# Filling the score operands in an attention-plus-MoE kernel: partition-to-partition DMAs replaced by VectorE copies

## The chip, the cores and the metric

The kernel runs on one core of a Trainium2 chip. The core has a matrix engine (TensorE, PE in the profile, with its weight loads listed as PEld), a vector engine (VectorE, DVE), a scalar engine (ScalarE, ACT), a general one (GpSimd, POOL) and SyncE (SP), which here only issues DMAs. Each engine works through its own queue in order. Sixteen DMA engines move data between HBM and the on-chip memory SBUF, or inside SBUF; matmul results land in PSUM. The metric is the device time of one execution in microseconds.

## The reference

For each of 4 x 8 heads, 768 queries of 64 numbers attend to keys in chunks of 32. A chunk's upper bound for a query comes from the chunk's smallest and largest key values, and only the six best chunks take part. The result goes through a dense two-layer network plus one of eight experts:

```
k_min = np.min(k_chunks, axis=3)
k_max = np.max(k_chunks, axis=3)
ub = np.sum(np.maximum(q[:, :, :, None, :] * k_min[:, :, None, :, :], q[:, :, :, None, :] * k_max[:, :, None, :, :]), axis=-1)
...
top_chunks = np.argsort(ub, axis=-1)[..., -top_k:]
scores = scale * np.matmul(q, k.transpose(0, 1, 3, 2))
...
mask = sel & (pos[:, None] >= pos[None, :])
scores = np.where(mask, scores, -1000000000.0)
...
h_dense = np.maximum(x @ w1_dense, 0.0)
y_dense = h_dense @ w2_dense
logits = x @ w_gate
expert_idx = np.argmax(logits, axis=1)
...
    h = np.maximum(x[mask] @ w1[e], 0.0)
    y_moe[mask] = gate_w[mask, None] * (h @ w2[e])
return (y_dense + y_moe).astype(np.float32)
```

## The kernel before, in words

Two heads of one batch make a pair, and there are 16 pairs. Head 0 of the pair has its 64 numbers on partitions 0 to 63 and head 1 on 64 to 127, since the two heads are transposed together. The masking of unchosen chunks is done inside the score matmul: it contracts over 128 rows, of which 64 carry the head's K and Q; of the other 64, 24 carry on Q's side a flag for each chunk that was not chosen, and on K's side, in 32 rows, -30000 where the key is in that chunk (the constant `exf`) and zeros below. So each head h of a pair has two operands, `kT[i][h]` for K and `rT[i][h]` for Q, in three sets i that take turns (`NB = 3`). In head 0's operands K and Q are on partitions 0 to 63 and the flags' part begins at 64; in head 1's it is the other way round.

A pair is prepared while earlier pairs are computed, in these steps:

- `cast_qk`, `cast_v`: GpSimd turns the loaded fp32 tiles into f16.
- `prep_k` (L379 on): TensorE transposes K into PSUM in six steps (L382); ScalarE copies the result into `kT[i][1]`, which thus holds both heads for a time (L384); VectorE takes the maximum and minimum of each chunk (L388) and builds `kb` (L391, L393), the operand of the upper bounds.
- `prep_q`: TensorE transposes Q (L405); ScalarE writes its positive part to `qp` (L408); VectorE copies it whole into `rT[i][0]` (L409); a DMA brings head 1's half to `rT[i][1]` (L410).
- `prep_kt`: a DMA copies head 0's half of `kT[i][1]` to `kT[i][0]` (L397), and then a second one overwrites rows 0 to 31 of `kT[i][1]` with `exf` (L398). The second has to wait until the first has read, and until the reduces have read.
- `prep_ub`: TensorE makes the upper bounds (L416, L420), using all of `rT[i][0]`; ten MAX8 instructions (L426) find the sixth best, and L428 writes flags.
- `prep_s`: TensorE transposes the flags (L434), VectorE copies them from PSUM to `se` in SBUF (L436), and two DMAs bring head 0's part to `rT[i][0]` (L438) and head 1's to `rT[i][1]` (L439).

The pair's work is then eleven units. In each, `scores` (L448) makes up to 512 columns of scores, ScalarE takes the exponential (L452), GpSimd cuts the diagonal in some units (L454), and `av` (L467) multiplies by V one unit later. `norm` divides and writes the MoE's input `xbig`. Scores of a pair run two units ahead of the loop, so the first scores of pair p + 1 are called at unit 9 of pair p. In the same loop run the fills: from the fifth pair on, pieces of the dense network of the previous batch (L242 to L331) are put between the units.

The loop says at which unit each step is called: `prep_s` of the next pair at unit 2, `prep_k`, `prep_q`, `prep_kt` and `prep_ub` of the pair after it at units 4, 5, 7 and 9. A scheduler in the framework then sets the order on each engine, so the final order is not quite that of the calls; it can be seen by comparing the built programs. SyncE issues all q, k and v loads, the writes of the dense results and the transfers named above through one queue in order. Loads have two buffers per tensor, so a load is issued once the cast two pairs earlier has freed its buffer. Transposes and upper bounds share two PSUM buffers, `pp`.

After the loop the tail gathers tokens by expert in 31 blocks, runs the two expert layers and scatters the rows out (L647 to L695).

Of the kernel before, what the change touches and what calls it, by code (L numbers as in the profile page):

```python
# [10 lines left out]
HF = mybir.dt.float16  # L11
# [6 lines left out]
def kernel(  # L18
# [12 lines left out]
    nc = tc.nc  # L31
    B, H, S, D = q.shape
# [40 lines left out]
    st = [dict() for _ in range(NP)]  # L73
# [23 lines left out]
    NB = 3  # L97
# [4 lines left out]
    kT = [[acst.tile([128, S], HF, name=f"kT{i}_{g}") for g in range(2)] for i in range(NB)]  # L102
    rT = [[acst.tile([128, S], HF, name=f"rT{i}_{g}") for g in range(2)] for i in range(NB)]
# [16 lines left out]
    exf = acst.tile([128, S], HF)  # L120
# [13 lines left out]
                            base=31, pattern=[[-1, S]], channel_multiplier=32)  # L134
    for i in range(NB):
        nc.vector.memset(kT[i][0][64:128], 0.0)
        nc.vector.memset(rT[i][1][0:64], 0.0)
        nc.vector.memset(v16[i][:, :, :, D : D + 1], 1.0)

    def expand(i):  # L140
        nc.scalar.copy(kT[i][0][64:96, :], exf[0:32])


    iom8 = const.tile([128, NT, E], FP)
# [211 lines left out]
    with (  # L356
# [21 lines left out]
        def prep_k(p):  # L378
            s = st[p]  # L379
            pk = pprep.tile([128, S], HF, name="pp")  # L380
            for t in range(NT):
                nc.tensor.transpose(pk[:, t * 128 : (t + 1) * 128], s["k16"][:, t].rearrange("p g d -> p (g d)"), ident)  # L382
            kp = kT[p % NB][1]
            nc.scalar.copy(kp.rearrange("d (T p j) -> d T p j", p=128, j=NJ),  # L384
                           pk.rearrange("d (T j p) -> d T p j", p=128, j=NJ))
            ks = ahead.tile([128, 2, NC], HF, name="ks")
            for i, op in enumerate((ALU.max, ALU.min)):
                nc.vector.tensor_reduce(out=ks[:, i], in_=kp.rearrange("d (c w) -> d c w", w=32), op=op,  # L388
                                        axis=mybir.AxisListType.X)
            s["kb"] = kb = ahead.tile([128, 3, 2, NC], HF, name="kb")  # L390
            nc.vector.tensor_tensor(kb[:, 0:2], ks.unsqueeze(2).to_broadcast([128, 2, 2, NC]),  # L391
                                    hmask.unsqueeze(1).to_broadcast([128, 2, 2, NC]), ALU.mult)
            nc.vector.tensor_tensor(kb[:, 2], ks[:, 1:2].to_broadcast([128, 2, NC]), nmask, ALU.mult)  # L393

        def prep_kt(p):
            k0, k1 = kT[p % NB]
            nc.sync.dma_start(out=k0[0:64], in_=k1[0:64])  # L397
            nc.sync.dma_start(out=k1[0:32], in_=exf[0:32])  # L398

        def prep_q(p):  # L400
            s = st[p]
            pq = pprep.tile([128, S], HF, name="pp")
            pqv = pq.rearrange("d (T h j p) -> d T h j p", h=2, j=NJ, p=64)
            for t in range(NT):
                nc.tensor.transpose(pqv[:, t // NJ, :, t % NJ], s["q16"][:, t].rearrange("p g d -> p (g d)"), ident)  # L405
            s["qp"] = qp = ahead.tile([128, S], HF, name="qp")
            r0, r1 = rT[p % NB]
            nc.scalar.activation(qp, pq, AF.Relu)  # L408
            nc.vector.tensor_copy(r0, pq)  # L409
            nc.sync.dma_start(out=r1[64:128], in_=r0[64:128])  # L410

        def prep_ub(p):

# [16 lines left out]
        def prep_s(p):  # L430
            s = st[p]
            ps = pprep.tile([128, S], HF, name="pp")
            for t in range(NT):
                nc.tensor.transpose(ps[:, t * 128 : (t + 1) * 128], fl[p % 2][:, t], ident)  # L434
            se = ahead.tile([128, S], HF, name="se")
            nc.vector.tensor_copy(se, ps)  # L436
            r0, r1 = rT[p % NB]
            nc.sync.dma_start(out=r0[64:96], in_=se[64:96])  # L438
            nc.sync.dma_start(out=r1[0:32], in_=se[0:32])  # L439

        def scores(p, u):
            s = st[p]
# [40 lines left out]
        for i in range(NB):  # L483
            expand(i)
        cast_qk(0)
        load(2, "kq")
        prep_k(0)
        prep_q(0)
        prep_kt(0)
        cast_v(0)  # L490
        prep_ub(0)
# [3 lines left out]
        load(2, "v")  # L495
        load(3, "v")
        prep_s(0)
        prep_k(1)
        prep_q(1)
        prep_kt(1)  # L500
        cast_qk(2)
        load(4, "kq")
# [19 lines left out]
        for i, (p, u) in enumerate(seq):  # L522
# [4 lines left out]
            if u == 2 and n1 is not None:  # L527
                prep_s(n1)
            if u == 4 and n2 is not None:
                prep_k(n2)  # L530
            if u == 5 and n2 is not None:
                prep_q(n2)
            if u == 7 and n2 is not None:
                prep_kt(n2)
# [214 lines left out]
```

## Time and profile before

The time was 357.41 us, the median of three runs (354.07 to 358.31). The profiled execution has a span of 337.3 us.

| | busy us | share of the span |
|---|---|---|
| PE | 244.4 | 72% |
| ACT | 173.6 | 51% |
| DVE | 165.7 | 49% |
| PEld | 156.8 | 46% |
| POOL | 154.0 | 46% |

| DMA inside SBUF, per pair | size of each | us to landing, median |
|---|---|---|
| kT<-kT, one | 96 KB | 4.6 |
| kT<-exf, one | 48 KB | 2.2 |
| rT<-rT, one | 96 KB | 4.1 |
| rT<-se, two | 48 KB | 5.4 |

Busy shares are averages over a prelude (up to the first score matmul at 23.9 us), the loop over pairs (up to about 227 us) and the tail, which have different limits, so they have to be read by stage. The landing time of a DMA counts from its issue; an engine that needs the data waits for the landing, and a DMA that is issued late lands late. In the lists of waits a line names the engine and line that stood, after the arrow what ended the wait, and then the microseconds in all, the number of waits and the longest. "out<-in" names tiles.

### The profile page before, as it was taken

What the parts mean: (1) busy time and instruction counts of PE and PEld (TensorE: products, weight loads), DVE (VectorE), ACT (ScalarE), POOL (GpSimd) and SP (SyncE); (2) the same over time, 40 slices, a digit from 0 to 9 for tenths busy, and PEclk for the clock granted to TensorE, in tenths of its full rate; (3) what the DMA queues carried; (4) which work ended last, traced back from release to release, by engine and by line L of the source; (5) the groups of instructions that cost most, each with busy time, mean ns of one, the idle gap of its engine ahead of it and who ended that gap; (6) DMA issues with size and microseconds to landing.
All of it is one profiled execution on the core that took longest, in us unless ns stands there. A gap on an engine that the chain in (4) does not pass through costs nothing.

```text
span 337.3 us, 7413 instructions
## 1 busy us (share of the span) xinstructions
PE 244.4 (72%) x2615; PEld 156.8 (46%) x2615; DVE 165.7 (49%) x556; ACT 173.6 (51%) x322; POOL 154.0 (46%) x203
## 2 busy tenths in 40 slices
PE   1418727849949859686686696989874998899882
PEld 1316516628616637454453473655441554444441
DVE  5526606527934447494352586237522454444441
ACT  4318707828817737558373664772341444444441
POOL 6635615436323514443424230110446677777753
PEclk9999958769978969799897989899995999999999
DMA  7976989797998798899994897223869578877760
GB/s 202 276 166 157 185 184 192 143 224 178 195 251 209 180 224 188 176 313 198 248 238 132 151 159 249 76 92 106 277 164 293 171 238 233 244 243 257 227 214 0
DMA packets 80499, 66.23 MB, mean 196 GB/s; under 512 B 30222, under 2 KB 73742, under 8 KB 80464
## 3 DMA queue, kind: packets, MB, share of 16 engines
q1 hardware_dynamic: 65280, 37.17, 40.2%
q0 software_dynamic: 15184, 28.60, 37.8%
q8 instruction: 21, 0.34, 0.4%
q14 instruction: 14, 0.11, 0.1%
HBM read 50.62 MB, written 20.91 MB: 212 GB/s over the span
## 4 chain that ended last, share of the span: by engine, by line
DMA 38%; PE 31%; issue 8%; DVE 8%; POOL 6%; ACT 4%; SPq 3%; POOLq 1%; ACTq 0%; DVEq 0%
DMA rT<-se 24%; PE sp L448 10%; DMA xg<-xd,gi 9%; PE yp L326 6%; POOL xg L647 3%; ACT ex L452 3%; DMA kT<-kT 3%; PE hp L317 3%; PE op L467 2%; POOL out_dram L695 2%; PE yp L691 2%; SPq L88 2%; PE hp L674 2%; PE pp L434 1%; DVE ks L388 1%
## 5 line engine op out<-in xcount | busy, mean ns | idle before, releaser
L452 ACT ACTIVATE ex<-sp 128x512 f16<-128x512 f32 (+1 forms) x176 | 92.6, 591 | 66.3 <-PE sp L448 63.0
L448 PE MATMUL sp<-rT,kT 128*128 128x128 f16 (+3 forms) x384 | 72.3, 297 | 46.8 <-DMA rT<-se 45.7
L454 POOL TENSOR_SCALAR_AFFINE_SELECT ex<-ex 128x512 f16<-128x512 f16 x48 | 31.8, 665 | 84.1 <-ACT ex L452 83.8
L448 PEld LDWEIGHTS <-kT 128*128 128x128 f16 x384 | 32.0, 109 | 56.3 <-issue 50.9
L467 PE MATMUL op<-v,ex 128*128 128x65 f16 x672 | 52.2, 201 | 8.0 <-ACT ex L452 4.7
L467 PEld LDWEIGHTS <-ex 128*128 128x128 f16 x672 | 39.7, 103 | 24.0 <-ACT ex L452 8.5
L695 POOL DMA_INDIRECT out_dram<-yo,si x31 | 31.4, 1013 | 16.0 <-DVE yo L694 9.3
L685 ACT COPY ehT<-tp 128x512 f16<-128x512 f16 x31 | 18.1, 585 | 36.9 <-PE tp L683 36.9
L388 DVE TENSOR_REDUCE ks<-kT 128x24 f16<-128x768 f16 x32 | 29.1, 947 | 14.7 <-ACT kT L384 13.9
L647 POOL DMA_INDIRECT xg<-xd,gi x31 | 29.8, 963 | 12.3 <-issue 5.8
L674 PE MATMUL hp<-we,exT 128*128 x124 | 31.8, 379 | 4.6 <-DVE exT L668 3.3
L691 PE MATMUL yp<-we,ehT 128*128 x124 | 32.7, 387 | 0.8 <-ACT ehT L685 0.8
L426 DVE MAX8 m<-pp 128x8 f32<-128x8 f32 (+4 forms) x160 | 16.0, 167 | 29.1 <-PE pp L420 28.9
L668 DVE COPY exT<-tp 128x512 f16<-128x512 f16 x31 | 13.1, 424 | 33.3 <-PE tp L666 33.3
L326 PE MATMUL yp<-wd,hT 128*128 128x512 f16 x96 | 28.9, 427 | 0.7 <-DVE ys L223 0.6
L317 PE MATMUL hp<-xT,wd 128*128 128x384 f16 x128 | 27.0, 330 | 1.1 <-ACT hT L319 0.3
L436 DVE COPY se<-pp 128x768 f16<-128x768 f16 x16 | 8.9, 557 | 37.3 <-PE pp L434 37.3
L694 DVE SCALAR_TENSOR_TENSOR yo<-yp,xg 128x512 f32<-128x512 f32 x27 | 20.3, 751 | 13.8 <-PE yp L691 12.0
L677 ACT ACTIVATE eh<-hp 128x512 f16<-128x512 f32 x31 | 18.5, 597 | 14.1 <-PE hp L674 14.1
L371 POOL CAST q<-qf 128x768 f16<-128x768 f32 x16 | 13.2, 824 | 25.9 <-DMA qf<-in_q_dram 19.0
L319 ACT ACTIVATE hT<-hp 128x384 f16<-128x384 f32 x32 | 15.8, 495 | 13.2 <-PE hp L317 7.5
L376 POOL CAST v<-vf 128x768 f16<-128x768 f32 x16 | 13.2, 827 | 17.5 <-PE op L467 12.8
(123 smaller groups left out, 386.0 us busy)
## 6 DMA issues: line engine op xcount, KB each, us to landing
we<-in_moe_w_dram POOLq DMA_DIRECT2D x16, 512.0 KB, 8.1
kf<-in_k_dram SPq DMA_DIRECT2D x32, 192.0 KB, 4.1
qf<-in_q_dram SPq DMA_DIRECT2D x32, 192.0 KB, 4.5
vf<-in_v_dram SPq DMA_DIRECT2D x32, 192.0 KB, 5.3
xd<-ys SPq DMA_DIRECT2D x24, 256.0 KB, 3.0
xo<-xbig SPq DMA_DIRECT2D x4, 792.0 KB, 6.7
xd<-xbig SPq DMA_DIRECT2D x4, 792.0 KB, 8.0
kT<-kT SPq DMA_DIRECT2D x16, 96.0 KB, 4.6
```

Source lines behind the costliest of these rows:

```text
L317: nc.tensor.matmul(hp, wd[:, ko, j * 128 : (j + 1) * 128], xT[:, ko, g * G * 128 : (g + 1) * G * 128], start=(ko == 0), stop=(ko == NK - 1))
L326: nc.tensor.matmul(yp, hold["h"][:, j, i * 128 : (i + 1) * 128], wd[:, NK + j], start=(j == 0), stop=(j == NK - 1))
L388: nc.vector.tensor_reduce(out=ks[:, i], in_=kp.rearrange("d (c w) -> d c w", w=32), op=op, axis=mybir.AxisListType.X)
L448: nc.tensor.matmul(sp[:, o : o + w], kT[p % NB][g][:, kt * 128 : (kt + 1) * 128], rT[p % NB][g][:, a * 128 : z * 128], start=(o == 0), sto ...
L452: nc.scalar.activation(ex[:, 0:o], sp[:, 0:o], AF.Exp, scale=0.125)
L454: nc.gpsimd.affine_select(out=ex, in_=ex, compare_op=ALU.is_ge, fill=0.0, base=0, pattern=[[0, 4], [1, 2], [2, 64]], channel_multiplier=-1)
L467: nc.tensor.matmul(s["op", g][:, t * (D + 1) : (t + 1) * (D + 1)], ex[:, o : o + 128], v16[p % NB][:, g, kt, :], start=first, stop=(last_o ...
L647: nc.gpsimd.indirect_dma_start(out=dst, out_offset=None, in_=src, in_offset=bass.IndirectOffsetOnAxis(ap=gi[:, i : i + 1], axis=0))
L674: nc.tensor.matmul(hp, s["xT"][:, ko], wef[:, bass.ds(offs[i] + ko * 512, 512)], start=(ko == 0), stop=(ko == NK - 1))
L691: nc.tensor.matmul(yp, s["hT"][:, j], wef[:, bass.ds(offs[i] + (NK + j) * 512, 512)], start=(j == 0), stop=(j == NK - 1))
L694: nc.vector.scalar_tensor_tensor(o, yp, s["x"][:, Dm : Dm + 2].bitcast(FP), s["y"], ALU.mult, ALU.add)
L695: sc = nc.gpsimd.indirect_dma_start(out=out, out_offset=bass.IndirectOffsetOnAxis(ap=si[:, i : i + 1], axis=0), in_=o, in_offset=None, bou ...
```

## The change

The flags leave PSUM straight for the operands, and no DMA moves data from partition to partition any more. It works because every copy now stays on its own partitions: the flags of head 0 are transposed to partitions 64 and up, where head 0's operand wants them, and those of head 1 to 0 and up.

K is now copied by ScalarE into a tile of its own, `kp`; VectorE copies head 0's half to `kT[i][0]` and head 1's to `kT[i][1]`. The `exf` rows are therefore written once, at the start, for both heads, and are never overwritten. VectorE also copies head 1's half of Q out of `rT[i][0]` before the flags go there, and then copies flags from PSUM to each operand, 64 partitions at a time, which also writes the zeros below the flags.

```
     for i in range(NB):
         nc.vector.memset(kT[i][0][64:128], 0.0)
-        nc.vector.memset(rT[i][1][0:64], 0.0)
+        nc.vector.memset(kT[i][1][0:64], 0.0)
         nc.vector.memset(v16[i][:, :, :, D : D + 1], 1.0)
 
     def expand(i):
         nc.scalar.copy(kT[i][0][64:96, :], exf[0:32])
+        nc.scalar.copy(kT[i][1][0:32, :], exf[0:32])
...
-            kp = kT[p % NB][1]
+            s["kp"] = kp = ahead.tile([128, S], HF, name="kp")
...
         def prep_kt(p):
-            k0, k1 = kT[p % NB]
-            nc.sync.dma_start(out=k0[0:64], in_=k1[0:64])
-            nc.sync.dma_start(out=k1[0:32], in_=exf[0:32])
+            kp = st[p]["kp"]
+            nc.vector.tensor_copy(kT[p % NB][0][0:64], kp[0:64])
+            nc.vector.tensor_copy(kT[p % NB][1][64:128], kp[64:128])
...
             nc.vector.tensor_copy(r0, pq)
-            nc.sync.dma_start(out=r1[64:128], in_=r0[64:128])
...
-            se = ahead.tile([128, S], HF, name="se")
-            nc.vector.tensor_copy(se, ps)
             r0, r1 = rT[p % NB]
-            nc.sync.dma_start(out=r0[64:96], in_=se[64:96])
-            nc.sync.dma_start(out=r1[0:32], in_=se[0:32])
+            nc.vector.tensor_copy(r1[64:128], r0[64:128])
+            nc.vector.tensor_copy(r0[64:128], ps[64:128])
+            nc.vector.tensor_copy(r1[0:64], ps[0:64])
```

## The prediction

> **What bounds the kernel now.** I read the chain that ended last first, to see which work sets the end; then the list of waits, to see how long each engine stood; then the timeline around one such wait, to see what it is made of; then busy time by stage, to see what would bind if the wait were gone.
>
> The chain, by engine and by line:
>
> ```profile
> DMA 38%; PE 31%; issue 8%; DVE 8%; POOL 6%; ACT 4%; SPq 3%; POOLq 1%; ACTq 0%; DVEq 0%
> DMA rT<-se 24%; PE sp L448 10%; DMA xg<-xd,gi 9%; PE yp L326 6%; POOL xg L647 3%; ACT ex L452 3%; DMA kT<-kT 3%; PE hp L317 3%; PE op L467 2%; POOL out_dram L695 2%; PE yp L691 2%; SPq L88 2%; PE hp L674 2%; PE pp L434 1%; DVE ks L388 1%
> ```
>
> A quarter of the span is the transfer of 48 KB of flags from se into rT; kT<-kT adds 3%. The waits (total, times, longest):
>
> ```profile
> ACT ex L452 <- PE sp L448: 63.0, 26, 8.3
> ...
> PE sp L448 <- DMA rT<-se: 45.7, 13, 7.3
> ...
> PEld L448 <- DMA kT<-kT: 2.9, 1, 2.9
> ```
>
> Tensor stands 45.7 us in 13 waits before the first score matmul of a pair, and Scalar's 63.0 us is mostly the same time seen one engine further. The first of the 13 is the prelude's 7.0 us (scores start at 23.9 us); 38.7 us lie in the pair loop. One of them, DVE, then SP's queue, then Tensor:
>
> ```profile
> 128.80 0.56 DVE L436 COPY se<-pp 128x768 f16<-128x768 f16 x1 [0.96 <-PE pp L434]
> ```
> ```profile
> 130.11 2.75 SPq L438 DMA_DIRECT2D rT<-se  x1
> ```
> ```profile
> 138.09 1.44 PE L448 MATMUL sp<-rT,kT 128*128 128x128 f16 x6 [3.52 <-DMA rT<-se]
> ```
>
> The copy ended at 129.4; SP reached the transfer at 130.1 and took 2.75 us to issue it; scores started at 138.1. The flags were ready 8.7 us before they could be used, and for the last 3.5 of these Tensor stood. By stage (prelude, pair loop, MoE tail; busy PE, PEld, DVE, ACT, POOL, then granted clock, DMA share, GB/s):
>
> ```profile
> 0.00:23.90 23.90, 5.63 (x50) 4.17 (x51) 11.43 (x43) 6.70 (x8) 13.82 (x33) 1.00 0.93 215
> 23.90:227.00 203.10, 151.57 (x1938) 107.43 (x1938) 106.31 (x403) 124.47 (x240) 75.00 (x104) 0.87 0.84 189
> 227.00:337.30 110.30, 87.15 (x631) 45.20 (x628) 47.95 (x111) 42.43 (x74) 65.18 (x66) 0.96 0.66 206
> ```
>
> In the loop Tensor idles 203.1 - 151.6 = 51.5 us, of which 38.7 is this wait. No other engine is above 124.5. DMA is not slack, though: share 0.84.
>
> **What the Trainium skill says.** "DMA: Bandwidth & Descriptors", Latency and other measured facts, gives a DMA some 2 us of fixed cost; section Issuing engines are not separate DMA queues says transfers of all queues interleave on the same 16 engines. The trace agrees: rT<-se lands in 1.9 us at best, but 5.4 at the median and 10.6 at worst. "VectorE: DVE Perf Modes", section The TRN2 errata, prices a copy at (120 + n/2)/0.96 ns from PSUM in 16 bit and (58 + n/4)/0.96 inside SBUF, with a measured fixed term nearer 150. For n = 768 from PSUM that is 525 ns; the trace has 548 and 557. "Advanced Engine Details and Errata", Mode Summary, says that Vector's second SBUF port is shared with GpSimd, so that fast SBUF copies and GpSimd work block each other. The trace agrees: the Am operation (L297) takes 308 ns at the median, but 807 where it runs beside GpSimd's cast of q. "TensorE: Matmul & The Clock Gate", Part 1, says that the clock halves after idle windows of about 3.4 us and comes back after as much activity; the loop's granted 0.87, against 1.00 in the stall-free 24 to 36 us, fits that.
>
> **The change, part by part.** Edits in each of the 16 pairs:
>
> Removed from SP: kT<-kT (96 KB), kT<-exf (48), rT<-rT (96), two rT<-se (48 each), 80 issues in all, and their waits. SP stood 26.6 us before kT<-exf alone, with q, k and v loads queued behind it. Bytes: 336 KB x 16 = 5.4 MB. At the loop's 189/0.84 = 225 GB/s per full share that is 24 us of DMA time, some 22 of it in the loop. The loop holds 0.84 x 203.1 = 171 us of DMA time, so 149 remain. From 4 to 18 us the prelude sustains shares of 1.08 to 1.29, so 149 can be done in about 125 us if asked.
>
> Removed from Tensor: 38.7 us of waits in the loop. The 2.9 us of kT<-kT is a weight load's wait inside the same stretches, so I don't add it.
>
> Added to Vector: two SBUF copies for K, one for Q (64x768 f16), and two PSUM copies for the flags in place of one. Half the partitions don't halve the time: the 64x384 memset of kT takes 378 ns, as the 128x384 one of fl does. PSUM: 0.557 more. SBUF copies aren't in the trace: 0.26 us by the price, 0.36 with the measured fixed term; the ceiling is the PSUM copy's 0.557. I take 0.30 plus nothing for the port, and keep 0.56 for the range. Sum 0.557 + 3 x 0.30 = 1.46 us a pair (1.3 to 2.2), 23 us in all, 22 in the loop: Vector goes from 106 to 128 us there, still below the new length. Most of it is hidden behind Tensor and Scalar.
>
> What is on the path: after the six flag transposes (L434), head 0's scores need only the copy into r0, 0.56 us plus a hand-off. In the changed order six K transposes and some ten attention-value matmuls stand between in most early pairs, 0.7 us by the timeline. The r0 copy has ahead of it on Vector the Q copy, which waits for the old r0 alone. Head 1's scores come five units later and hide the second copy. The K copies stand before the ten MAX8 (L426): 0.6 us added on the way to the flags. Who waits behind them: MAX8, flags, transposes. Also, with the waits gone, Tensor will meet kb later than it wants: K transposes, Scalar's copy (0.80), two reduces (1.81), kb (0.3) make 3 us, partly covered by scores that Scalar paces at 0.5 us a unit. I charge 0.7 us of new waits a pair for all this, 11 us (0 to 30).
>
> Given back by the clock: 151.6 us of Tensor work at 0.87. At 0.97 it would be 136, 15 less. Scalar's 124.5 is close by then, so I count 12.
>
> Loop: 203.1 - 38.7 + 11 - 12 = 163 us, 40 less. Scalar would be 76% busy, Vector 79%, DMA share 0.91.
>
> Prelude: Scalar now makes six copies of exf instead of three before K's first copy: 3 x 0.825 = 2.5 us later. Against that, flags are in se at 15.6 and scores start at 23.9, 8.3 later. With 2.5 us of Scalar, 0.9 of K and Q copies and 0.1 for hand-off, scores start near 15.6 + 3.5 = 19: 5 us won. kT's cleared rows and the dropped memset of rT cancel. The tail is the same instructions: 0.
>
> Sum: 40 + 5 = 45 us from the span. The timed median is 357.4 against 337.3 profiled; I take those 20 us as unchanged, and add 2 us of gain, in case part of them is in the waits: 357.4 - 47 = 310.
>
> **The rivals.**
> *Vector becomes the pacer.* The reduces, MAX8, normalisation and now 1.46 to 2.2 us more stand in one in-order queue, and every flag needs several of them in turn. For it: 128 us, or 139 at 0.56 a copy, in 163 us. Against: Vector stands 37.3 us for L434 alone now, time that came from the same stall. If each pair then waits 2 us for Vector rather than 0.7, 20 us are lost: 330.
> *DMA or the loads become the pacer.* For it: GpSimd already waits 19.0 us for qf, longest 5.7, and shares pass 1 at 140 to 180 us. Against: SP no longer stands before the loads, and 22 us of traffic go. If the share stays at 0.84, the loop is 149/0.84 = 177: 324.
> *All gives way.* The clock stays at 1.00 and new waits vanish; the loop goes to 203 - 39 - 18 = 146, 57 us less, 62 with the prelude: 293 with the same 2.
> *Slower.* The wait moves: Tensor stands for Vector as long as it did for DMA, because K's copies and the port shared with GpSimd delay the flags. To be slower, the new waits must eat the whole 38.7 + 12 + 5 + 2 = 58 us, 3.9 a pair. Only a bad order gives that; at 4.4 a pair the time is 310 - 11 + 66 = 365. Little speaks for it: what is put in the place of a 9 us hand-off takes 0.56.
>
> **How the numbers follow.** Forecast 0.60 (310), Vector 0.14 (330), loads 0.10 (324), all gives way 0.10 (293), no change 0.02, slower 0.04. The range runs from 291, at which the cheapest copies and full clock still stand, to 333, which holds Vector at the dear price. Faster by over 2% (below 350) 0.94; same 0.02; slower 0.04.
>
> **What would show it.** Right: no DMA row with rT or kT as its destination; score matmuls wait for DMA nowhere; first scores near 19 us; pair loop near 163 us at a clock over 0.92; the three SBUF copies near 0.3 us, PSUM ones 0.55; the DMA share near 0.9. Wrong: a new large wait of score matmuls for the r0 copy, or of L420 for kb (Vector), or of GpSimd for qf, kf and vf beyond 19 us (loads); SBUF copies much over 0.36 us (port). The prediction fails most easily in the new waits: Tensor, Scalar, Vector and DMA all come to between 75 and 90% of the loop, and in-order queues seldom run so full.

## The result and the profile after

The changed kernel takes 304.3 us (median of four, 303.8 to 306.6) against 357.1 before: the ratio is 0.854, 95% interval 0.848 to 0.860. The forecast was 310.

The chain that ended last, by engine and by line, now reads:

```profile
PE 40%; DVE 26%; ACT 11%; issue 10%; POOL 5%; DMA 5%; another core or an unknown queue 1%; POOLq 1%; ACTq 0%; SPq 0%; DVEq 0%
PE yp L690 8%; PE hp L673 7%; PE sp L447 5%; PE hp L318 4%; ACT ex L451 4%; DVE ks L389 4%; PE yp L327 4%; DVE m L426 3%; DMA xd<-ys 2%; POOL out_dram L694 2%; DVE rT L436 2%; DVE xbig L477 2%; PE tp L665 2%; PE tp L682 2%; PE op L466 2%
```

DMA fell from 38% of the chain to 5%, VectorE rose from 8% to 26%, and no single line has more than a tenth. What the score matmuls still wait for (total, times, longest):

```profile
PEld L447 <- issue: 9.2, 26, 1.0
...
PE sp L447 <- ACT ex L451: 3.7, 7, 0.9
```

The 45.7 us behind a DMA have become 3.7 us behind the exponentials of earlier units. By stage: prelude, loop up to the last score matmul, the stretch from there to the first expert matmul, expert stage (columns as before: length, busy PE, PEld, DVE, ACT, POOL, granted clock, DMA share, GB/s):

```profile
0.00:18.68 18.68, 4.54 (x43) 3.44 (x44) 10.50 (x42) 7.65 (x9) 11.62 (x30) 1.00 1.02 236
18.68:171.21 152.53, 135.86 (x1923) 97.28 (x1923) 138.42 (x467) 122.63 (x239) 78.66 (x107) 1.00 0.99 217
171.21:190.97 19.76, 17.15 (x163) 9.52 (x160) 12.66 (x51) 7.52 (x16) 3.92 (x4) 1.00 0.60 202
190.97:304.90 113.93, 84.07 (x492) 43.36 (x491) 35.19 (x61) 36.55 (x62) 61.25 (x63) 0.85 0.53 169
```

The loop went from 203.1 us (201.8 if it, too, is counted only up to the last score matmul) to 152.5, and scores start 5.2 us sooner. In the loop TensorE is busy for 89% of the time, VectorE for 91%, ScalarE for 80%, and the DMA share is 0.99: where one wait ruled, several resources are now close to full. But the expert stage, counted from its first matmul, is 113.9 us where the profile of before had 92.8, with the same instructions. That had to be settled first, and a further profile of before did it:

```profile
0.00:23.71 23.71, 5.63 (x50) 4.16 (x51) 11.44 (x43) 6.70 (x8) 13.77 (x33) 1.00 0.94 215
23.71:222.45 198.74, 152.63 (x1924) 109.58 (x1924) 105.96 (x402) 124.12 (x239) 75.05 (x104) 0.87 0.87 193
222.45:241.31 18.86, 15.49 (x156) 8.72 (x152) 12.05 (x50) 6.64 (x14) 3.93 (x4) 1.00 0.57 190
241.31:350.40 109.09, 78.59 (x492) 41.99 (x491) 35.45 (x61) 35.87 (x62) 61.26 (x62) 0.89 0.56 177
```

Here before itself has an expert stage of 109.1 us and a span of 350.4 (its first score matmul stands at 23.95, a little behind the cut at 23.71). So before has been seen with expert stages of 93 to 95 and of 109, and the changed kernel only with 109 to 114. A stage of the long kind explains most of the 20 us between before's first profile (337.3) and its timed median (357); an execution of 357 itself wasn't profiled. Like is compared with like by setting this second profile of before against one of the changed kernel with an expert stage of 110.9: prelude 24.0 to 19.1, loop and the stretch behind it 217.4 to 171.9, span 350.4 to 301.9, which is 48.5 us less, and 45.5 of it lie between the first score matmul and the first expert matmul. I use that stretch, called the middle below, to compare kernels, since the expert stage varies. It comes from one profile per kernel; the three of before differ by 3.3 us in it, the three of after by 0.5.

### The profile page after: what moved, and what is told of

Its sections match the earlier page's. It is cut to its first block, busy times and chain, and to the rows that moved or that the text cites. A ratio compares the mean times of both kernels' runs of the same rounds, so it can differ in the third digit from the quotient of the medians.

```text
span 304.9 us, 7337 instructions
## 1 busy us (share of the span) xinstructions
PE 241.6 (79%) x2615; PEld 153.6 (50%) x2615; DVE 196.8 (65%) x620; ACT 174.4 (57%) x325; POOL 155.4 (51%) x203
## 4 chain that ended last, share of the span: by engine, by line
PE 40%; DVE 26%; ACT 11%; issue 10%; POOL 5%; DMA 5%; another core or an unknown queue 1%; POOLq 1%; ACTq 0%; SPq 0%; DVEq 0%
PE yp L690 8%; PE hp L673 7%; PE sp L447 5%; PE hp L318 4%; ACT ex L451 4%; DVE ks L389 4%; PE yp L327 4%; DVE m L426 3%; DMA xd<-ys 2%; POOL out_dram L694 2%; DVE rT L436 2%; DVE xbig L477 2%; PE tp L665 2%; PE tp L682 2%; PE op L466 2%
## 5 line engine op out<-in xcount | busy, mean ns | idle before, releaser
L447 PE MATMUL sp<-rT,kT 128*128 128x128 f16 (+3 forms) x384 | 63.9, 261 | 6.6 <-ACT ex L451 3.7
L466 PE MATMUL op<-v,ex 128*128 128x65 f16 x672 | 45.7, 193 | 2.0 <-DVE xbig L477 1.0
L673 PE MATMUL hp<-we,exT 128*128 x124 | 37.1, 428 | 9.7 <-DVE exT L667 5.8
L466 PEld LDWEIGHTS <-ex 128*128 128x128 f16 x672 | 35.5, 97 | 13.4 <-POOL ex L453 2.8
L676 ACT ACTIVATE eh<-hp 128x512 f16<-128x512 f32 x31 | 18.5, 597 | 28.8 <-PE hp L673 14.9
L389 DVE TENSOR_REDUCE ks<-kp 128x24 f16<-128x768 f16 x32 | 29.3, 941 | 7.9 <-ACT kp L385 7.8
L318 PE MATMUL hp<-xT,wd 128*128 128x384 f16 x128 | 26.1, 324 | 2.8 <-DVE rt L283 1.3
L327 PE MATMUL yp<-wd,hT 128*128 128x512 f16 x96 | 24.6, 378 | 0.7 <-DVE ys L224 0.3
L370 POOL CAST k<-kf 128x768 f16<-128x768 f32 x16 | 13.2, 824 | 19.6 <-PE pp L383 16.6
L673 PEld LDWEIGHTS <-exT 128*128 128x128 f16 x124 | 12.5, 108 | 20.5 <-issue 7.8
L690 PEld LDWEIGHTS <-ehT 128*128 128x128 f16 x124 | 12.3, 107 | 16.5 <-issue 7.4
L385 ACT COPY kp<-pp 128x768 f16<-128x768 f16 x16 | 12.9, 805 | 10.2 <-PE pp L383 10.2
```

The costliest lines, as they stand in the source:

```text
L318: nc.tensor.matmul(hp, wd[:, ko, j * 128 : (j + 1) * 128], xT[:, ko, g * G * 128 : (g + 1) * G * 128], start=(ko == 0), stop=(ko == NK - 1))
L327: nc.tensor.matmul(yp, hold["h"][:, j, i * 128 : (i + 1) * 128], wd[:, NK + j], start=(j == 0), stop=(j == NK - 1))
L447: nc.tensor.matmul(sp[:, o : o + w], kT[p % NB][g][:, kt * 128 : (kt + 1) * 128], rT[p % NB][g][:, a * 128 : z * 128], start=(o == 0), sto ...
L466: nc.tensor.matmul(s["op", g][:, t * (D + 1) : (t + 1) * (D + 1)], ex[:, o : o + 128], v16[p % NB][:, g, kt, :], start=first, stop=(last_o ...
L673: nc.tensor.matmul(hp, s["xT"][:, ko], wef[:, bass.ds(offs[i] + ko * 512, 512)], start=(ko == 0), stop=(ko == NK - 1))
L690: nc.tensor.matmul(yp, s["hT"][:, j], wef[:, bass.ds(offs[i] + (NK + j) * 512, 512)], start=(j == 0), stop=(j == NK - 1))
```

## The experiments

| kernel | time, before beside it | ratio (95%) | first scores | middle | expert stage |
|---|---|---|---|---|---|
| before, three profiles | | | 23.7 to 24.0 | 217.3 to 220.6 | 92.8, 95.3, 109.1 |
| after, three profiles | 304.0, 354.9 | 0.853 (0.844 to 0.862) | 18.7 to 19.2 | 171.8 to 172.3 | 108.6 to 113.9 |
| flags' part alone | 313.8, 339.8 | 0.926 (0.916 to 0.936) | 20.8 | 198.7 | 93.0 |
| K's and Q's part alone | 332.3, 339.8 | 0.980 (0.968 to 0.992) | 26.1 | 208.3 | 93.1 |
| after + traffic, real sources | 317.4, 339.8 | 0.936 (0.925 to 0.948) | 19.3 | 201.1 | 94.6 |
| after + traffic, constant source | 337.4, 357.2 | 0.945 (0.935 to 0.955) | 18.5 | 203.2 | 110.7 |
| after, SBUF copies on GpSimd | 307.5, 354.9 | 0.864 (0.857 to 0.871) | 22.0 | 173.1 | 110.9 |
| after, SBUF copies twice | 318.8, 354.9 | 0.896 (0.887 to 0.905) | 20.0 | 185.6 | 111.4 |
| after, SBUF copies left out from the fourth pair on | 299.2, 357.2 | 0.833 (0.823 to 0.843) | 19.0 | 169.0 | 111.0 |
| after, exf copies later | 305.1, 354.9 | 0.858 (0.851 to 0.865) | 13.9 | 178.2 | 114.0 |

All columns but the ratio are in us. Times stand beside those of before taken with them on the same chip. For K's and Q's part alone the interval reaches 0.992, so by the time alone its gain is not clear; the middle has to carry that reading.

**Before and after once more.** No edits. The first time, before gave 339.6 us and an expert stage of 95.3:

> The kernel before, unchanged, profiled once more. In the profile of before the span was 337.3 us but the timed median was 357; in the profile of after the span (304.9) equals the timed median (304). The pair loop shrank by 50 us (203.1 to 153.3) and the prelude by 5, yet the expert stage grew by 24 us (91.3 to 114.9). Theory A: the short expert stage of 91 us was peculiar to that one execution of before, and usual executions of before have one of about 110 us, so this profile shows a span near 355 with loop near 203 and expert stage near 110. Theory B: the expert stage really became slower by the change (its weights, gathers or TensorE's clock), so this profile shows about 91 us there again, and the 20 us between span and time lie elsewhere, for example in a longer loop.

> After, unchanged, beside before on the chip of this call, for comparison with the other kernels. On another chip before took 339.8 us with an expert stage of about 92 us. Theory A (the change shortens only the prelude and the pair loop; the slow expert stage in the first profile of after belongs to that chip and would be there for before too): the gain is the same 50 us or so in microseconds on any chip, and the expert stages of both kernels are equal within 3 us. Theory B (the change itself slows the expert stage): on a chip where before's expert stage is about 92 us, this one's is near 115.

> After, unchanged, once more, for comparison with the other kernels of this call. So far before took 339.8 us (expert stage 92 us) on one chip and 354.9 on another, and after was seen only on the second, with an expert stage of 111 to 115 us. Theory A (the slow expert stage belongs to the chip): if before takes some 340 us here, after's expert stage is near 92 us and its time near 288; if before takes some 355, after takes 304. Theory B (the change slows the expert stage): 111 us or more on any chip, so about 304 here even if before takes 340.

> Before, unchanged, once more, for its stages. After has shown expert stages of 108.6 to 114.9 us on chips where before's time is 355 to 357; before's stages are known only from executions of 337 and 336 us, with expert stages of 91 to 95 us. Theory A (the slow expert stage belongs to the chip): if the time here is 352 us or more, the pair loop is near 203 us all the same and the expert stage is 105 to 112; if the time is near 340, the stages are those already seen. Theory B (the change slows the expert stage): the expert stage is 91 to 95 us whatever the time, and a time of 352 or more would come from the pair loop.

The first expectation fell on neither side: the execution was again one of the short ones, and so was the time. After gave 304.0 us beside a before of 354.9, then 305.5 beside 357.2, with expert stages of 110.9 and 108.6; the condition of the second and third expectations, a before near 340 beside it, never came up. The last one went against theory B: a time of 352.1 us, middle 217.4, and an expert stage of 109.1. Before has both lengths, so the long stage doesn't need the change; and after with the transfers put back (below) had a stage of 94.6, so it doesn't follow from it either. Nor does it belong to the chip, as theory A had it: the record gives the same chip for the 95.3 of the first run and the 109.1 of the last.

**One half at a time.** First, flags from PSUM alone:

```
-            se = ahead.tile([128, S], HF, name="se")
-            nc.vector.tensor_copy(se, ps)
             r0, r1 = rT[p % NB]
-            nc.sync.dma_start(out=r0[64:96], in_=se[64:96])
-            nc.sync.dma_start(out=r1[0:32], in_=se[0:32])
+            nc.vector.tensor_copy(r0[64:128], ps[64:128])
+            nc.vector.tensor_copy(r1[0:64], ps[0:64])
```

> Before with the flags' part of the change alone: two PSUM copies into the score operands, K's and Q's copies still by DMA. Theory A (the late flag transfer is the bound): most of the 53 us come, about 312 to 320 us; the Q transfer now has to be read out before VectorE may write the flags, which costs a little. Theory B (the SyncE queue and the traffic of all five transfers are the bound, the flags only show it): the wait moves to the K or Q transfer, 335 to 350 us.

313.8 us: two fifths of what the whole change brings in the middle (18.6 of 45.5). The time fits theory A's numbers, but the wait did move, as theory B had it. VectorE now stands at the flag copy, since the Q transfer must have read head 1's half of r0 first:

```profile
DVE rT L436 <- DMA rT<-rT: 40.9, 11, 8.8
...
PE pp L405 <- DVE rT L437: 11.5, 4, 7.8
PE sp L446 <- DVE rT L436: 11.3, 7, 4.8
```

Of the 40.9 us of waiting on VectorE, TensorE paid 11.3 before scores and 11.5 before transposes of Q, which stand behind the late flag copy (L437). Then the other half, K and Q by VectorE with the flags still by DMA:

```
-            nc.vector.tensor_copy(r0[64:128], ps[64:128])
-            nc.vector.tensor_copy(r1[0:64], ps[0:64])
+            se = ahead.tile([128, S], HF, name="se")
+            nc.vector.tensor_copy(se, ps)
+            nc.sync.dma_start(out=r0[64:96], in_=se[64:96])
+            nc.sync.dma_start(out=r1[0:32], in_=se[0:32])
```

> After with the flags still copied to se and brought over by the two 48 KB DMAs: K's and Q's part of the change alone. Theory A (flag transfer is the bound): score matmuls go on waiting for the flag DMAs, though these are issued sooner since SyncE no longer stands for K's transfer; 335 to 345 us. Theory B (SyncE's queue and the traffic): most of the gain is here, 310 to 320 us.

332.3 us, a little under theory A's range, and the wait for the flags is there still, shortened from 42 to 36 us:

```profile
PE sp L450 <- DMA rT<-se: 35.8, 13, 5.6
```

So theory A holds for what TensorE waits for. But 18.6 and 9.0 make 27.6, not 45.5: the halves help each other, and 18 us of the gain come only when both are made.

**The traffic without the waits.** The five transfers are issued in the changed kernel as before, with the same sizes and from the same queue, into scratch tiles:

```
+            sa = ahead.tile([128, S], HF, name="sa")
+            nc.sync.dma_start(out=sa[64:128], in_=kp[0:64])
+            nc.sync.dma_start(out=sa[0:32], in_=exf[0:32])
...
+            sb = ahead.tile([128, S], HF, name="sb")
+            nc.sync.dma_start(out=sb[0:64], in_=r1[64:128])
+            nc.sync.dma_start(out=sb[96:128], in_=r0[64:96])
+            nc.sync.dma_start(out=sb[64:96], in_=r1[0:32])
```

> After, with the five transfers per pair issued all the same (same sizes, same queue) into scratch tiles that no engine reads. Theory A (only waiting for them cost time): within 2% of after, 304 to 310 us. Theory B (their traffic and their place in SyncE's queue cost time, since the DMA share in the loop is 0.99 already): GpSimd waits for q, k and v loads grow well over the present 10 us and the time is 318 us or more.

Theory A fell. No engine needs the data of these transfers (the list of waits has one wait for them, of 0.5 us), and yet the middle is 201.1 us, 29 more than after, with GpSimd's wait for the K loads at 28.2 us. (The 317.4 us lie just under theory B's 318, but with an expert stage of the short kind.) Either SyncE stood for the sources with the loads behind it, or the transfers cost as such. In the next kernel every source is a constant tile, so that no engine has to be waited for:

```
-            nc.sync.dma_start(out=sa[64:128], in_=kp[0:64])
-            nc.sync.dma_start(out=sa[0:32], in_=exf[0:32])
+            nc.sync.dma_start(out=sa[64:128], in_=czero[0:64])
+            nc.sync.dma_start(out=sa[0:32], in_=czero[32:64])
...
-            nc.sync.dma_start(out=sb[0:64], in_=r1[64:128])
+            nc.sync.dma_start(out=sb[0:64], in_=czero[64:128])
...
```

> After, with five transfers per pair of the same sizes from a constant tile into scratch tiles that no engine reads: unlike in the earlier traffic kernel their data is there from the start, so SyncE never has to stand for ScalarE or VectorE before it can issue them, and the loads behind them aren't held up by that. In the earlier one (22 us faster than before, where the whole change brought about 50) GpSimd waited 28 us for K loads. Theory A (the transfers cost by their place in the queue: SyncE waits for their sources while loads stand behind): within 5 us of after. Theory B (they cost as traffic and as issues, each takes a place among the DMAs in flight): 15 us or more slower than after, with GpSimd waiting over 20 us for loads again.

337.4 against 305.5 us for after beside it: theory B. GpSimd's wait for the K loads, in the changed kernel and then in this one:

```profile
POOL k L370 <- DMA kf<-in_k_dram: 3.0, 4, 1.4
```
```profile
POOL k L372 <- DMA kf<-in_k_dram: 49.8, 11, 9.4
...
PE op L475 <- POOL ex L462: 25.4, 10, 4.5
```

The second line of this kernel shows TensorE behind GpSimd in turn.

The DMA share was near 1 and stayed there; the loops, first that of after (the profile taken beside it), then that of this kernel:

```profile
19.15:170.84 151.69, 135.44 (x1915) 97.25 (x1915) 137.85 (x467) 122.17 (x238) 78.54 (x107) 1.00 0.98 217
```
```profile
18.49:201.58 183.09, 144.87 (x1915) 103.84 (x1915) 141.97 (x467) 123.28 (x238) 78.81 (x107) 0.92 0.96 211
```

0.96 x 183.1 - 0.98 x 151.7 = 27 us of DMA time are added for 16 x 336 KB = 5.4 MB, and that loop is 31 us longer. So the transfers cost by being there; how they do it stays open between two readings. One is bytes, as in this sum. The other is SyncE's own time: its issuing takes 62 of the 152.5 us of after's loop (first profile) and 147 of the 183 here. In this kernel the two K loads of a pair, from the seventh pair on, are out 13.5 to 21.0 us after their buffer came free, against 0.9 to 2.1 us in after, and for most of that SyncE is issuing what stands ahead. But an issue has no fixed price: the kernel below without SBUF copies has after's transfers and spends 102 us on them. A third reading, a limit on transfers in flight, explains little: in the traces of before and of the kernel with real sources SyncE never has more than eight in flight, but it stands for a landing for only 5.6 us with real sources and 5.4 us here (the wait at the very end left out).

**Is VectorE the new pacer?** The three SBUF copies a pair were doubled, then given to GpSimd, then left out:

```
+            sa = ahead.tile([128, S], HF, name="sa")
+            nc.vector.tensor_copy(sa[0:64], kp[0:64])
+            nc.vector.tensor_copy(sa[64:128], kp[64:128])
...
+            sb = ahead.tile([128, S], HF, name="sb")
+            nc.vector.tensor_copy(sb[64:128], r0[64:128])
```

> After with the three SBUF copies per pair made twice, the second time into scratch tiles that no engine reads: 48 more VectorE copies of 64x768 f16, 0.36 us each, 17 us of work. Theory A (VectorE paces the loop): 10 to 17 us slower than after. Theory B (VectorE's copies lie in slack, as the prediction had it): under 5 us slower.

```
-            nc.vector.tensor_copy(kT[p % NB][0][0:64], kp[0:64])
-            nc.vector.tensor_copy(kT[p % NB][1][64:128], kp[64:128])
+            nc.gpsimd.tensor_copy(kT[p % NB][0][0:64], kp[0:64])
+            nc.gpsimd.tensor_copy(kT[p % NB][1][64:128], kp[64:128])
...
-            nc.vector.tensor_copy(r1[64:128], r0[64:128])
+            nc.gpsimd.tensor_copy(r1[64:128], r0[64:128])
```

> After with the three SBUF copies per pair (two for K, one for Q) made by GpSimd. Theory A (VectorE with 138 of 153 us is the busiest engine of the loop and its chain paces it): VectorE drops to about 118, GpSimd rises from 79 to some 115; 4 to 8 us faster than after. Theory B (VectorE isn't the pacer, or GpSimd's queue with its waits for loads is a worse place): same or up to 10 us slower, with score matmuls or VectorE waiting for GpSimd's copies. The start of the scores may come later, since GpSimd is behind with casts in the prelude.

```
+            if p < NB:
                 nc.vector.tensor_copy(kT[p % NB][0][0:64], kp[0:64])
                 nc.vector.tensor_copy(kT[p % NB][1][64:128], kp[64:128])
...
+            if p < NB:
                 nc.vector.tensor_copy(r1[64:128], r0[64:128])
```

> After without VectorE's three SBUF copies from the fourth pair on, so that those pairs compute their scores with K of both heads, and Q of head 1, of an earlier pair: 39 copies of 0.36 us, 14 us of VectorE work left out and moved to no other engine. Theory A (VectorE's chain paces the loop): 7 to 12 us faster than after. Theory B (VectorE is one of several engines that are nearly full, TensorE 137, VectorE 138, ScalarE 123 of 153 us, DMA share 0.99): under 4 us.

The loops of the three, in this order:

```profile
20.04:185.43 165.39, 141.38 (x1916) 99.04 (x1916) 155.45 (x512) 122.95 (x239) 80.13 (x107) 0.99 0.90 198
```
```profile
22.00:175.01 153.01, 136.70 (x1923) 99.04 (x1923) 123.41 (x423) 123.93 (x239) 112.99 (x151) 0.98 0.98 212
```
```profile
19.02:168.47 149.45, 135.87 (x1919) 97.95 (x1919) 120.58 (x427) 123.47 (x239) 77.48 (x107) 0.98 1.01 222
```

Doubling adds 17.6 us to VectorE (155.5 against 137.8) and 13.7 to the middle: more work here is paid for the most part. Moving 14 us to GpSimd frees none, though GpSimd's busy time rises from 79 to 113 us with it. Leaving 17 us out frees 2.8 us of the middle, but the time is 299.2 against 305.5 for after beside it, 6 us less, and one profile doesn't show where the rest lies. So VectorE has little left, and something else is not far behind it: with VectorE at 121 us the DMA share is 1.01 at 222 GB/s, and TensorE is at 136 of 149 us. Theory A held for the first kernel and theory B for the second; the third lies between its two theories. That DMA is what holds the last one is a reading of its share; a kernel with fewer bytes to load wasn't tried.

**A shorter prelude.** ScalarE's six copies of exf go behind its first copies of K and Q:

```
-        for i in range(NB):
-            expand(i)
...
         prep_q(0)
+        expand(0)
         prep_kt(0)
...
         prep_q(1)
+        expand(1)
+        expand(2)
         prep_kt(1)
```

> After with ScalarE's six copies of exf placed behind its first copies of K and Q in the prelude, instead of ahead of them. K's first copy then starts about 4 us earlier at the most. Theory A (the prelude is a chain of K cast, copy, reduces, flags, so the six copies delay the first scores by the 2.5 us that were predicted for three of them and as much again for the other three): first scores near 15 us instead of 18.7, and 2 to 4 us off the time. Theory B (loads hold the prelude): same.

Scores start at 13.9 instead of 19.1, more than expected, and the time doesn't move. TensorE then stands for GpSimd, which casts V only when its load is there, first in GpSimd's timeline and then in TensorE's:

```profile
19.74 0.82 POOL L377 CAST v<-vf 128x768 f16<-128x768 f32 x1 [2.40 <-DMA vf<-in_v_dram]
...
21.29 0.67 POOL L453 TENSOR_SCALAR_AFFINE_SELECT ex<-ex 128x512 f16<-128x512 f16 x1
```
```profile
22.02 0.40 PE L466 MATMUL op<-v,ex 128*128 128x65 f16 x4 [5.25 <-POOL ex L453]
```

In after the first of these matmuls runs at 22.3. Loads hold the start: theory B. The sooner start only became a pause of 5 us, and the granted clock from 13.9 to 40 us was 0.87, against 1.00 in after. No version tried here that computes everything beats the changed kernel.

## Why the prediction was right, and where it was off

*The wait.* Right as far as TensorE's own waits go. The 38.7 us behind the flag transfer were real and are gone, and nothing of their size took their place. "I charge 0.7 us of new waits a pair for all this, 11 us (0 to 30)" was too much: TensorE's idle time in the loop up to the last score matmul, the old wait left out, went from 12.3 to 16.7 us, 4.4 more.

*The clock.* Right in kind. TensorE's busy time in the same stretch fell from 150.9 to 135.9 us, 15.0 less, where 12 were counted; the granted clock is 1.00. In these terms the loop went 201.8 - 38.7 + 4.4 - 15.0 = 152.5. This has to come out, since busy and idle time make up the loop; it says where the forecast of 163 was too long, by 7 us of new waits, 3 of clock and 1 of the loop's end, and not why the waits stayed small.

*VectorE's cost.* Mis-sized. I took "0.30 plus nothing for the port". The rows of after, with min, median and max in ns, from the Q and flag copies and then the K copies:

```profile
L436 DVE COPY rT<-rT x16: 354/358/1749, 15.4 to 159.8; 64x768 f16<-64x768 f16 x16
L437 DVE COPY rT<-pp x16: 560/561/562, 18.1 to 161.2; 64x768 f16<-64x768 f16 x16
L438 DVE COPY rT<-pp x16: 549/550/551, 18.7 to 161.8; 64x768 f16<-64x768 f16 x16
```
```profile
L398 DVE COPY kT<-kp x16: 308/342/873, 14.7 to 156.2; 64x768 f16<-64x768 f16 x16
L399 DVE COPY kT<-kp x16: 357/357/511, 15.1 to 157.0; 64x768 f16<-64x768 f16 x16
```

The PSUM copies are as forecast. The SBUF copies have about the dear one of the two prices, 0.36 us, and beside GpSimd more than that: the two K copies average 0.42 and 0.37, the Q copy 0.62, one of the signs of being wrong that the forecast named. In all that is 1.97 us a pair instead of 1.46. One of its long ones, and GpSimd at that time:

```profile
118.98 1.75 DVE L436 COPY rT<-rT 64x768 f16<-64x768 f16 x1
```
```profile
119.20 1.31 POOL L453 TENSOR_SCALAR_AFFINE_SELECT ex<-ex 128x512 f16<-128x512 f16 x2
```

It ends 0.2 us after GpSimd's two selects, which agrees with the Trainium skill's "Advanced Engine Details and Errata", Mode Summary, by which GpSimd and VectorE's copies that use both SBUF ports block each other. VectorE's busy time rose by 31.1 us in all, not 23. "Most of it is hidden" held as far as it was needed, for leaving the copies out gains 3 us (by the middle) to 6 us (by the time); but there is little room left, as the doubled copies show.

*DMA.* The amount was right and its role was wrong. "So 149 remain" became 0.99 x 152.5 = 151 us. But I counted the removed 22 us of DMA time as relief that is worth nothing by itself, and wrote 0 for it in the sum. The two traffic kernels show that with those transfers in place, and with no engine waiting for their data, 29 to 31 us of the middle's 45.5 are lost again. My sum would have given the kernel with the constant source the same 310 us, and it takes 337: that the number for the change came near is in part luck, since one change removed both the wait and the transfers. The old loop's DMA share of 0.84 to 0.87 was no slack for a loop 46 us shorter. My forecast of a share of 0.91 came out as 0.99, since the loop got shorter than forecast. The same kernels make the wait alone worth about 14 to 16 us in the middle once traffic is put back, though waits and traffic can't be added: the first hid the second.

*The prelude.* Right about the start: scores start at 18.7 us; forecast 19. Whether that is worth the 5 us that the sum gave it is not shown, for in the kernel with the later exf copies 5 us more of the same kind brought nothing.

*The tail and the 20 us.* The tail's instructions are the same, and against before's long expert stage they took as long, 108.6 to 113.9 us beside 109.1. "I take those 20 us as unchanged" came out without the forecast knowing what they were. A time exceeds its own span by under 2 us (339.06 and 337.3 for the first profile of before). As far as the profiles show, the 20 us were mostly a longer expert stage in the timed executions; both kernels have it, so it drops out of the difference.

*The rivals.* None came to pass as a whole. VectorE as pacer and loads as pacer each appear one step away, in the doubled copies and in the traffic kernels.

## What to carry to other kernels

When one wait is removed, ask of every resource how full it would be in the shorter loop, and test a shared one like DMA by putting its removed load back without its wait. Here a copy between partitions by DMA cost its consumer a landing time between 1.9 and 10.6 us (48 KB of flags in before), and held up the loads that share DMA engines and SyncE's queue with it; where the data could be produced on the partitions that need it, a vector copy straight from PSUM took 0.56 us. Before a span is subtracted from a span, compare the stages that the change doesn't touch.

## What the runs showed of the hardware that was not expected

The expert stage, with the same instructions, took 93 to 95 us in some executions and 109 to 114 in others, of before alone as well. In the long ones the granted clock is 0.85 to 0.89, against 0.91 to 0.96, and DMA moves 169 to 178 GB/s, against 202 to 209. What makes it long is open.

Averaged over the loop, a mix of loads in rows of 256 and 512 bytes, weights and results moved 211 to 222 GB/s in all kernels with a DMA share near 1, whatever was added or removed. It is no ceiling: in stretches of 20 us between 20 and 140 us of its second profile, after moved between 215 and 253 GB/s at shares of 1.00 to 1.14. Those kernels that averaged under 200 GB/s were, by their waits and busy times, held by something else: by the flag wait in before and in K's and Q's part alone, and by VectorE where its copies were doubled.
